# Two layers of decode attention and MLP: the streamed head pairs of a row grouped into one job of four

## The chip, the cores and the metric

One core of one Trainium2 chip. The metric is the device time of the kernel in microseconds (us). Executions of one kernel lie within about 0.5% of their median here. Before and after are compared with the runs that were taken beside each other. A program on one core has no second die to be compared with, so a run counts as fast when it lies within 1.5% of the fastest of its kernel.

## The reference

```python
W = min(4096, max(256, Sk // 4))           # 1024 of 4096 keys
q = (x @ wq).reshape(B, 1, 32, 128)        # 8 rows, 32 heads of 128, width 640
scores = einsum("bhqd,bhkd->bhqk", q, k[last W]) * 128 ** -0.5
o = einsum("bhqk,bhkd->bhqd", softmax(scores), v[last W])
attention = o.reshape(B, 1, 4096) @ wo

x = x + attention(layernorm(x))            # layer 1
x = x + mlp(layernorm(x))                  # 640 -> 1728, gelu, -> 640
x = x + attention(layernorm(x))            # layer 2: the SAME K and V, the same weights
x = x + mlp(layernorm(x))
```

Two things matter. The second layer reads the same K and V as the first, so whatever stays on the chip need not be loaded twice. And a row's second layer cannot begin before that row's first attention is complete and has gone through output projection, MLP, layernorm and query: a serial chain of small steps, once for each of the 8 rows.

## The kernel before

K or V of one *pair* of heads of one row is one unit of 128 x 2048 bf16 (512 KB). There are 27 unit buffers in SBUF. A row has 16 pairs, so 32 units; pairs 5 to 15 are kept for the second layer, pairs 0 to 4 are loaded again ("streamed"). Pair 5 is kept in PSUM instead of SBUF ("parked"), so 20 kept units lie in SBUF and 7 of the 27 buffers circulate.

```python
NUNIT = 27
STREAM = ((0, 3), (3, 5))                       # jobs whose K and V are loaded in both layers
KEEP = ((5, 8), (8, 12), (12, 16))              # jobs whose K and V stay for the second layer
PARK = {b: (('k', 5), ('v', 5)) for b in range(8)}
NOT = {}
WINDOWS = ("0:1a 0:1b 0:2a 0:2b", "1:0a 0:3a 0:3b", ..., "1:5a 1:5b 1:6a 1:7a 1:6b 1:7b")
ORDER = ( ... )                                 # a long string: the order in which all steps are emitted
```

A *job* is a group of up to four pairs that share one score bank, one exponent, one set of transposes and one set of folds. The tile `scr`, which takes the result of the exponent and later the sums of the folds, exists once for all jobs; the prediction calls it "the one score buffer". `WINDOWS[b]` lists the streamed jobs that are worked off while row b's chain runs ("1:0a" is layer 2, row 0, the first streamed job). The last window holds what waits for the last chain. In outline, one job is:

```python
def scores(job, i):      # 4 matmuls a pair; the K buffer comes free here, if it is not kept
    nc.tensor.matmul(job.s_ps[...], lhsT=view(low, ...), rhs=k[:, 512*a:512*a+512], ...)
    release(job, "k", i)
def exponent(job):       # one for the whole job
    nc.scalar.activation(scr[:], job.s_ps[:], ACT.Exp, scale=QSCALE)
def turn(job): ...       # 4 transposes (PE), then place() copies them (ACT), totals(), inverse()
def values(job, i):      # 4 matmuls a pair; the V buffer comes free here
    nc.tensor.matmul(job.o_ps[...], lhsT=view(misc, ...), rhs=v[:, 512*g:512*g+512], ...)
    release(job, "v", i)
def fold(job, t): ...    # 4 on DVE, then halve() twice, gathered() 2 matmuls, finish()
```

`chain(b)` is the MLP of row b, its layernorm and its queries. Every load is issued by one queue in a fixed order and waits until the next buffer of the free list is free.

The softmax here doesn't subtract the row's maximum and nothing guards it: scores larger than these inputs give would overflow.

Of the kernel before, what the change touches and what calls it, by code (L numbers as in the profile page):

```python
# [18 lines left out]
H = 32  # L19
# [3 lines left out]
F = 1728  # L23
EPS = 1e-5
QSCALE = DH ** -0.5
NKC = D // P
# [2 lines left out]

UNIT = 2048  # L30
NUNIT = 27
STREAM = ((0, 3), (3, 5))
KEEP = ((5, 8), (8, 12), (12, 16))
PARK = {b: (('k', 5), ('v', 5)) for b in range(8)}
ALSO = {}
NOT = {}
WINDOWS = ("0:1a 0:1b 0:2a 0:2b", "1:0a 0:3a 0:3b", "1:0b 1:1a 0:4a 0:4b", "1:1b 0:5a 0:5b", "1:2a 1:2b 0:6a 0:6b",
           "1:3a 1:3b 0:7a 0:7b", "1:4a 1:4b", "1:5a 1:5b 1:6a 1:7a 1:6b 1:7b")
WINDOWS = [[(int(w[0]), int(w[2]), ord(w[3]) - 97) for w in x.split()] for x in WINDOWS]
WPOS = (("w1", -1), ("w2", -1), ("wo", 8))  # L40
NHC = 13
HALF = F - NHC * P
ORDER = (
    "I))%(z<&2/,@/-%)%9yxyxyxyxyx2.z*z,z,z,y`y`y`z),,(4y[%yZyZyZ)zIy[y[yYyZyZyZyZyZyYyY&-(y[y[y]z9/&yTyT)+*(&(yRyqy"
    "RypyRyRyRyRyRyRyjyj&yVyXyVyYyYyYyYyYyYyYyYyYy]y]y]y]y_y_ykykyk{.{.yWyWyZyVyTyfyf{&yYyY{8yYyU{6yMyWyWyWyWyVy[y^"
    "y[y]y]%y_yU$#yQyQ$##yNyNyNzfzfyGyHyHyHyHyJyGyIyKz]yKz[z[yHyGzY#yFyFyFyFyFyFyF#z^yFyF$yMyDyDyDzVzgyDzHzH%yCzQzF"
    "%yByBzCzCzZyDyBzIzWzW#ziyAyAz>z>z>z>yAyAyAz`#z:y@y@y@zHz<$yAz8z9zCz3zRzBy?z2##z4y>z3z3z3y>z2z1z.z0z6y>#-&$z+yN"
    "z;z/z:z-yNy:z,y:yLyLy~&6)#z#z#z#z#z#z)y6yzy}y`y|/y5y}y~y~y5#y|yuyuyzyzyzyYy4yByUyUyByBysyryryr+yRypyRyq,##yOy2"
    "y2y2y;y;y0y1y9#%$#&y,yXy,y,y,y,y+y<y<yVy<y+y/y/y-yHyHy+yGy7#$#y*y*y2yDyGy*y*yBy*yXy*y&y)y,y,y>yjy,y)y+y+y)y*y8"
    "y8y8yIyIyIy8y]yHy*y*y*y3y/y*y(y)y)y0#%%##y#y,y,##y4y4y4y4y*y*x|y)x}y(x|y<y<y.y&y#$y$zVy$y6x~y&x}y3x~y$y$y$y/x~"  # L50
    "zJzJzJy#y#y,y#y#y#y#x}x~x~x~z?%y$zLx}x|##x|xzxzxzx}z4xzxzz2z?xzxzxzxzz;z.xzxzxzxz##z4xyxyxxz1xxz#xxz?x~y}y}$xx"
    "z)xwyzxwxwyxyxyxyxz1xyxwyzz.#y{xvxvxvxvyqxvyp#ys#&yoxsylynxsxvyvyvxvxsxsxt2$yfyoxnxqxqxqxqy&%y_y_y_y_y_$&#%yZ%"
    "#&y]xzxiyXxiyXxxxxxiyUyUyUyUy2yTyTxiy/y/xvxvxjxu%)yKxh-+xfxfxdy%y?y>x~y=xmxm$%xkx{x{y1y1y1xcxcxcxcxcxhxfxcxqxc"
    "y+yHxpxpxe#xdy)xdy($+xjxjxxxj$x~xwxaxa#xfy3y3xwx`x_x_%xcx^x^xqxazbxlx`x^x_xlxlxlx_x_x_x_x_zUxxxgx_x^xezP##&xb("
    "xcxYxmxWy#xZxXx_#xhxTxgx]x]x]x]x]x]xYxY#xoxoxoxo%x]xXx^x[xjxjx]x]x]x[z6xSxW#%xWz1xUxVxVxVxV#xZx]xTxTxTz%yrxWxX"
    "ypy}%#z0xRxQxQxQxQxQxTxMxPyrxPydz#xPxPxPxPxP#y`yixO#y[ytxNxNxNxNxNxNyVyVyVxNxKyZxM#yfyRyRyRyRyTxLxPySyPxLyQyZ$"
    "yYxNyOxKygygygxKyU#yLxK#xIxIyHyHyHyHyHyL#>&.$xDxDxDxDyCyAxGyAy>yJxGxDxDxEy7y7xE&yBxDxDy6y?y6y6y67y5y5xUxCy7xTx"
    "ky1y5y5*#&xQy,y/x@x@-+x|x|-#xzx<y$y$y$y$xJxJxJxJx|xwxxx_x_#x;&xrxyxYxsx;x;x;xUxoxVxUxpx;xCxCx7xexBx:x:*xMxMx?x"
    "9x9$####xYx4x4x6x3x1x@x4x4x4x2x3x;x;x;xOx;x3x3xzx3x3x3x3xHx6xtx5x3x4x4x3xVxBxBxBx;xRxRxRxRx3x3x3x>x3x3x3##)x9x"
    ";x0x:$xC#x6z,x-x5x?x?#x4x1x2xKxKxK#x,x0x0x0x0x0x4x/%x3x3x.x2ynx2x.x*x:%x9x,x8&yex7x-x-x&x,x,x2yKx+x+x+yHyHx+yj"  # L60
    "x+x-x-x+x,yBx/x*x*x*x*x*x*yIy;x*x*y9yE#yU###x%y4x%y>yNx%#yLx&x&x*yIx$x$x$x$x$y*y*y2$y)y)y)y)x(y,y(y(x#x&y%%w~w"
    "~x#w~x~x~x~x~y,x~x~x~y)w~-<9y%w{w{$wzwzxu,wy*xxwxwywywywywywywyxoxixgxhxhx/xjx/x/x/x/9wwxd##$x]x`x`wqx_zsx_x)x"
    "^x;wsxSzmzm)#$)%$wmw|wmzdwozcwmwmxNwmwmwmxMx,wuwuxA)#$wjxExGxG$wiwixqwiwiwiwkwywkwlwlwlwlwix9wvwsx7wux6x,wgx2w"
    "jwjwjwgwgxWwowox+whwhx:x+x-wgwgwgx%x###wfw|x#wgwgwuw|wuwgx?wzwzwzwzx#wgw~w~wyx6w}wvwgwfwv##*+wbwbwb#wq##)wnwnw"
    "nw^w^w]w]wgy<w]wdw]w`wtw]yVwa#y4#wbwbwZwawawkwkwkwkw^yHw`y(y(w`w`w`w`w^w_#w]y=wbw]w]w`w]w_wbw^wYw[w[w^xoxow[xn"
    "y-w]%y+wZ#y:xlwYwYwYwYxhw[xew[x{wYwYwbwYxa#y*x`x`x`x`x`x`$xawWwXx_wXwWx]wWx[x[xYwYxbwW#xWxWxWxWxWwWwVxhxZ###%3"
    "wQwQxNwQxQxOxMxZwQxNwQwQxVwSwSwQwRwRwRwRwRxDxD#xAxAxAxAxAxFxAx=wcwcxBx>xBxBx;wQ&wPw`w`w`)w_w_(3#0&$x<x2x;x1x,x"
    "-x/x/#wkx-x-x-wHwEwiwix)wgwgwUwUx(wGwHwHwHwGwG#(#%wKwywZwCwCwCwCwCwFwTwTwTwGwjwAwBwEwOwBwBwCw{wLwCwKwCwCwCwHw_"
    "wCwG+wRwWyMwGwGwBwBwBwD-wKwQwQwQwKwCwCwCwCwCwCw[w[$wZwZ&##*$w?w:wDwF#y?wAw;wC$#w7wJwJw9wIx}x}x}w=w>w>w>w>wF#w="
    "w=wAw=wAwAwAw;w?w<wHxkxkwH&w;()w:w6w9w9w3w8w8w7xlw7xkw;w;w7w:w7w6w2w4w4#w4w4w4w6w4w4xjw3w3w3w3w5w3w4w3xRxDx`w3"  # L70
    "w1xrw2w2x[x@w2xKxX#xWw1w1w2w1w1w1w1w1#%x5x5#w.xIw.w.x1w0x8w.xSx/x/x/x/x/x/x1w/w/x/w.#x-x-x+w-$#x)x)w+x(w+x&x;x"
    "+#w*w*xHx#x#x(x%w-w,w*#w{w}w(x,w)x+w{w(w($.%+x#w#wkwkw|w#w#w#wowowowowowmwn*$,()#w/w/wfwjwjwGwGw/wfqq#wcwCwCpw"
    "`w`w`w`w`w+w+$#w<w<nw(w(oow7wSwMoow#w#&w2vnnnwHnw-w-wE(#pw=lolnnlmmw9#(#rrrw3w5##hw2hhwDwDhhhhkkw*hvwQw(hiwNwN"
    "h%&&ueoeeow.eneew*w*nhejkll#ettiw1w1#rhhhegggcekkehdhh#c#oooeeeebjjbb_%#x+]]cccf]bb]]]#_wx_[#wuwuZZx(ZZZZ$#wmw"
    "mwmwzZZ^wj$]wiwiwrWWZWYWwlYwyWWw`whWXwf#w]w]w]w]w]VVV#)XwVwewZwXTTTTwUwRTTwRwRwRTwNwPwPwNwOwSTTTT%$$$$#)wD__MM"
    "MwBwBOO)Lw>MMUmw6UUw7UUMMwDMMMM(#$a^^w)JKw(w*w*]]u[KqrvvsuuZZw%ZKmppMKnLLL%###%DDw*MM#ZcccDDD]%CCCEGCDREESSSEE"
    "x1EB````OMDDDDKKKKJCGRRRDQGGGwq%#EBKKJDCCCCECDABDDBCA##$wW>>>>>wRwcwR@@wP>>>w[w[>wLwY###wI<wT<wHwHwH##::99wW:;"
    "wH$wSw?w?w?w?wE8w>w>88#7w<w:777w9788w6w6w68w:8888%)#)wvw*w+w+w+w+%/#)w&^^[[AA000r22(o;1/l08j0wV0-wU555FF/////]"
    "A[[[[00RRW0Q#(##$PPPO999LL#$&`$))F&((0CB0A0(((<(((99#)*&))333))))</--9...-)$($&(>(#&&&#88%%%@?F%J%%2E;(:1%#$$-"
    "-;$$$$$-$3#0&(++%+#*)$##$#")  # L80


class Job:
# [59 lines left out]
def _kernel(ctx: ExitStack, tc: tile.TileContext, A_small, A_k, A_v, A_wq, A_wo, B_w1, B_w2, out):  # L143
# [46 lines left out]
    xn = single["yT"]  # L190
# [30 lines left out]
    x0 = in_sb[:, 0:NKC * NB].rearrange("p (k b) -> p k b", b=NB)  # L221
# [365 lines left out]
    def add_job(job, early, rank0, ask=None, tail=False):  # L587
# [8 lines left out]
        def keep_apart(which, i, use):  # L596
            if job.layer == 0 and (which, i) in PARK.get(job.b, ()):
                for k in range(2):
# [4 lines left out]
        if job.layer == 1:  # L603
            src = twin(job)
            for w, i in PARK.get(job.b, ()):
                if i in pairs:
# [117 lines left out]

    held = {(w, i) for w in "kv" for i0, i1 in KEEP for i in range(i0, i1)}
    rows = []
    for b in range(NB):
        at, h = {}, (held | set(ALSO.get(b, ()))) - set(NOT.get(b, ()))
        rows.append([{part: [Job(b, layer, i0, i1, h, at) for i0, i1 in cut]
                      for part, cut in (("s", STREAM), ("k", KEEP))} for layer in range(2)])  # L730

# [8 lines left out]
    xn8 = narrow(NKC, NB, "xn8")  # L740
    _, _, r8 = layernorm(direct, x2, NB, lambda: xn8, False, "ln_r")
    q8_bank, q8_ps = bank(H, NB)
    for h in range(H):
        for kc in range(NKC):
            nc.tensor.matmul(q8_ps[:, h, :], lhsT=wq_sb[:, kc, h * DH:(h + 1) * DH],
                             rhs=xn8[:, kc, :], start=(kc == 0), stop=(kc == NKC - 1))
    nc.vector.tensor_tensor(out=qo, in0=q8_ps.rearrange("p h b -> p b h"), in1=r8()[:, :, None].to_broadcast([P, NB, H]),
                            op=ALU.mult)
    give(q8_bank)
# [16 lines left out]
    def late():  # L766
        first = asked[0]
        ends = []
        for part in range(len(STREAM) + len(KEEP)):
            at = [(x[1]["s"] + x[1]["k"])[part] for x in rows]  # L770
# [16 lines left out]
                         after=[d for d, h0, h1 in ends if h0 < h + 2 and h1 > h] + [head], take="park" if h == 0 else None)  # L787
            head = head or t

    jobs = rows[0][0]["s"] + rows[0][0]["k"]  # L790
    for b in range(NB):
        for layer, row, k in WINDOWS[b]:
            jobs = jobs + [rows[row][layer]["s"][k]]
        jobs = jobs + [job for job in rows[b][1]["k"] if any((w, i) not in job.held for w in "kv" for i in range(job.i0, job.i1))]
        jobs = jobs + (rows[b + 1][0]["k"] if b + 1 < NB else [])
# [7 lines left out]
    extra = {}  # L803
    for name, pos in WPOS:
        if pos < 0:
# [51 lines left out]
    y8 = narrow(NKC, NB, "y8")  # L857
# [43 lines left out]
```

## Time and profile before

| | before |
|---|---|
| time, median of the runs (their range) | 491.48 us (491.18 to 492.07) |
| span of the profiled execution | 488.7 us |
| PE busy | 392.6 us, 80% |
| DVE busy | 256.2 us, 52% |
| ACT busy | 76.4 us, 16% |
| loads on the queue | 191.13 MB, of which 336 units |
| last load lands / attention ends | 469.0 / 478.1 us |

The prediction shows the page's slices, the stretches, the landings and the groups. Three readings carry the rest: DMA moves 417 GB/s in nearly every slice, so the load stream is full; a few slices dip, all of them where a chain runs; and the last two slices have almost no loads (91 and 4 GB/s; the last one lands at 469.0), so something other than the loads fills the end.

### The profile page before, as it was taken

How to read it: one execution, taken by the hardware profiler on the slowest of the kernel's cores; microseconds unless marked ns; L12 is line 12 of the kernel's file. 1: busy time of each engine (PE TensorE's matmuls, PEld its weight loads, DVE VectorE, ACT ScalarE, POOL GpSimd, SP SyncE). 2: the span in 40 equal slices, each digit the busy share in tenths (PEclk: the TensorE clock that was granted, in tenths of full speed). 3: DMA queues.
4: the chain of work that ended last, by engine and by line, in shares of the span. 5: the costliest groups of instructions: out<-in, count | busy, mean ns of one | idle time of the engine just before them, and what ended most of it. 6: DMA issues, size and time to landing. Idle time of an engine off the chain costs nothing.

```text
span 488.7 us, 16784 instructions
## 1 busy us (share of the span) xinstructions
PE 392.6 (80%) x7201; PEld 212.3 (43%) x7201; DVE 256.2 (52%) x1116; ACT 76.4 (16%) x195; POOL 12.7 (3%) x24
## 2 busy tenths in 40 slices
PE   1412645998899998898989989988999899889985
PEld 0300124553365436542564355535552464365354
DVE  3001422455735764477454755666466746757563
ACT  1000000111211111112111211112112111121220
POOL 1000000000000000000000000000000000000001
PEclk9996555556655755557555575587556655765765
DMA  8999999999999999999999999999999999999920
GB/s 328 417 420 420 438 421 417 418 417 418 416 418 415 416 416 420 402 411 419 418 380 403 417 417 411 412 419 414 416 416 417 418 373 392 416 415 414 417 91 4
DMA packets 49898, 192.20 MB, mean 393 GB/s; under 512 B 5792, under 2 KB 5792, under 8 KB 48800
## 3 DMA queue, kind: packets, MB, share of 16 engines
q1 hardware_dynamic: 49824, 191.13, 96.5%
q8 instruction: 56, 0.92, 0.7%
q14 instruction: 18, 0.15, 0.1%
HBM read 191.10 MB, written 0.01 MB: 391 GB/s over the span
## 4 chain that ended last, share of the span: by engine, by line
PE 53%; DMA 21%; DVE 17%; issue 4%; ACT 3%; POOLq 0%; ACTq 0%; SPq 0%; DVEq 0%
PE s_ps L435 13%; PE o_ps L476 12%; DMA unit<-in_A_k_dram 9%; PE c_ps L536 6%; PE c_ps L698 6%; DMA unit<-in_A_v_dram 6%; DVE scr L486 5%; DMA wo_sb<-in_A_wo_dram 4%; PE c_ps L450 3%; PE c_ps L319 3%; PE o_ps L511 2%; PE c_ps L359 2%; PE c_ps L500 2%; DVE scr L484 2%; PE c_ps L273 1%
## 5 line engine op out<-in xcount | busy, mean ns | idle before, releaser
L435 PE MATMUL s_ps<-unit,low 128*1 128x512 bf16 (+3 forms) x1024 | 123.5, 564 | 18.9 <-DMA unit<-in_A_k_dram 13.2
L476 PE MATMUL o_ps<-unit,misc 128*8 128x512 bf16 (+3 forms) x888 | 108.2, 555 | 12.9 <-DMA unit<-in_A_v_dram 6.8
L444 ACT ACTIVATE scr<-s_ps 128x512 bf16<-128x512 f32 x80 | 47.8, 597 | 217.7 <-PE c_ps L500 127.9
L486 DVE SCALAR_TENSOR_TENSOR scr<-o_ps,low,scr 128x128 f32<-128x128 f32 x213 | 74.1, 348 | 5.9
L484 DVE TENSOR_SCALAR scr<-o_ps,low 128x128 f32<-128x128 f32 x71 | 24.7, 348 | 46.7 <-PE c_ps L450 30.1
L536 PEld LDWEIGHTS <-wo_sb 128*128 128x128 bf16 x1280 | 38.4, 103 | 21.5 <-issue 14.3
L435 PEld LDWEIGHTS <-low 128*1 128x1 bf16 (+3 forms) x1024 | 22.6, 91 | 50.3 <-issue 34.8
L698 PEld LDWEIGHTS <-wq_sb 128*128 128x128 bf16 x1280 | 38.0, 102 | 13.4 <-issue 12.6
L698 PE MATMUL c_ps<-low,wq_sb 128*128 128x1 bf16 x1280 | 40.8, 165 | 0.8 <-ACT misc L454 0.4
L454 ACT CAST misc<-c_ps 128x48 bf16<-128x48 f32 (+2 forms) x80 | 21.8, 272 | 123.0 <-DVE misc L465 22.1
L476 PEld LDWEIGHTS <-misc 128*8 128x8 bf16 (+3 forms) x888 | 20.2, 91 | 38.6 <-issue 27.1
L450 PEld LDWEIGHTS <-scr 128*128 128x128 bf16 x320 | 15.1, 104 | 39.9 <-ACT scr L444 35.7
L500 PEld LDWEIGHTS <-scr 128*128 128x128 bf16 x142 | 11.7, 105 | 39.1 <-DVE scr L495 12.2
L450 PE MATMUL c_ps<-misc,scr 128*128 128x16 bf16 x320 | 21.1, 176 | 8.7 <-ACT scr L444 5.7
L536 PE MATMUL c_ps<-misc,wo_sb 128*128 128x1 bf16 x630 | 19.8, 165 | 7.5 <-DMA wo_sb<-in_A_wo_dram 5.1
L465 DVE TENSOR_REDUCE misc<-c_ps 128x8 f32<-128x64 f32 (+2 forms) x80 | 16.0, 200 | 17.9 <-PE c_ps L460 11.6
L319 PEld LDWEIGHTS <-w_sb 128*128 128x128 bf16 x675 | 20.4, 104 | 9.9 <-issue 9.4
L460 PE MATMUL c_ps<-misc,low 128*128 128x48 bf16 (+2 forms) x80 | 16.5, 206 | 9.8 <-ACT misc L454 7.0
L500 PE MATMUL c_ps<-low,scr 128*128 128x8 bf16 x142 | 17.5, 176 | 7.6 <-DVE scr L493 3.3
L427 DVE CAST low<-c_ps 128x6 bf16<-128x6 f32 (+2 forms) x56 | 8.5, 154 | 28.0 <-ACT misc L454 16.9
L536 PE MATMUL c_ps<-low,wo_sb 128*128 128x1 bf16 x650 | 20.9, 165 | 2.3 <-DVE misc L465 1.4
L495 DVE TENSOR_TENSOR scr<-scr 128x128 bf16<-128x128 f32 x71 | 20.3, 286 | 2.4 <-PE s_ps L435 0.2
(98 smaller groups left out, 305.4 us busy)
## 6 DMA issues: line engine op xcount, KB each, us to landing
unit<-in_A_v_dram SPq DMA_DIRECT2D x168, 512.0 KB, 9.2
unit<-in_A_k_dram SPq DMA_DIRECT2D x168, 512.0 KB, 9.0
wq_sb<-in_A_wq_dram SPq DMA_DIRECT2D x5, 1024.0 KB, 8.9
wo_sb<-in_A_wo_dram SPq DMA_DIRECT2D x1, 5120.0 KB, 21.3
w_sb<-in_B_w_dram SPq DMA_DIRECT2D x1, 2176.0 KB, 25.1
w_sb<-in_B_w_dram SPq DMA_DIRECT2D x1, 2160.0 KB, 29.0
unit<-in_A_small_dram SPq DMA_DIRECT2D x1, 15.0 KB, 1.7
out_dram<-unit SPq DMA_DIRECT2D x1, 10.0 KB, 1.4
```

The costliest lines, as they stand in the source:

```text
L319: nc.tensor.matmul(t["h", k][1][:, fc - halves[k][0], :], lhsT=w_sb[:, kc * F + c0:kc * F + c0 + P], rhs=t["y"][:, kc, :], start=(kc == 0) ...
L435: nc.tensor.matmul(job.s_ps[32 * a:32 * a + r + 1, :], lhsT=view(low, job.qz + 5 + d - (d + 1) * r, (d + 1, r + 1)), rhs=k[:, 512 * a:512 ...
L444: nc.scalar.activation(scr[:], job.s_ps[:], ACT.Exp, scale=QSCALE)
L450: nc.tensor.matmul(job.t_ps[1][:, c], lhsT=scr[:, c * P:(c + 1) * P], rhs=small_ident.rearrange("p (a r) -> p a r", a=4), start=True, stop ...
L454: nc.scalar.copy(view(misc, 0, (64, job.n), (1, 4), (4, 4)), job.t_ps[1][:, :, :, 0:job.n].rearrange("p t a i -> p i a t"))
L476: nc.tensor.matmul(job.o_ps[32 * g:32 * g + 4 * r + 4, :], lhsT=view(misc, 48 * r + g, (4, 4 * r + 4)), rhs=v[:, 512 * g:512 * g + 512], s ...
L484: nc.vector.tensor_scalar(out=acc, in0=o[:, 0], scalar1=mask[:, 0:1], scalar2=None, op0=ALU.mult)
L486: nc.vector.scalar_tensor_tensor(out=acc, in0=o[:, t], scalar=mask[:, t:t + 1], in1=acc, op0=ALU.mult, op1=ALU.add)
L495: nc.vector.tensor_tensor(out=parts[:, 1], in0=acc, in1=parts[:, 0], op=ALU.subtract)
L500: nc.tensor.matmul(job.o8[1], lhsT=parts[:, h], rhs=sel, start=(h == 0), stop=(h == 1))
L536: nc.tensor.matmul(sums[1][:, n:n + 1], lhsT=wo_sb[:, h, n * P:(n + 1) * P], rhs=job.ot[:, h - 2 * job.i0:h - 2 * job.i0 + 1], start=(h == ...
L698: nc.tensor.matmul(job.q_ps[1][:, h - 2 * job.i0:h - 2 * job.i0 + 1], lhsT=wq_sb[:, kc, h * DH:(h + 1) * DH], rhs=xn[:, kc, :], start=(kc ...
```

## The change

Intent: one streamed job of four pairs instead of one of three and one of two, so 4 jobs for each row and layer, not 5 (64, not 80). With each job goes one exponent, one set of transposes, four folds and one gather. To keep the same number of units in SBUF, pair 5 now belongs to a kept job but is loaded again all the same, and pair 4 is kept in its place.

```diff
-STREAM = ((0, 3), (3, 5))
-KEEP = ((5, 8), (8, 12), (12, 16))
-PARK = {b: (('k', 5), ('v', 5)) for b in range(8)}
+STREAM = ((0, 4),)
+KEEP = ((4, 8), (8, 12), (12, 16))
+PARK = {b: (('k', 4), ('v', 4)) for b in range(8)}
-NOT = {}
-WINDOWS = ("0:1a 0:1b 0:2a 0:2b", "1:0a 0:3a 0:3b", ..., "1:5a 1:5b 1:6a 1:7a 1:6b 1:7b")
+NOT = {b: (('k', 5), ('v', 5)) for b in range(8)}
+WINDOWS = ('0:1a 0:2a', '0:3a', '0:4a 1:0a', '0:5a 1:1a', '0:6a 1:2a', '0:7a 1:3a', '1:4a', '1:5a 1:6a 1:7a')
+EARLY = [... for w in ''.split()]              # empty: no effect
 ORDER = ( ... )                                # another order string, cut here
@@ the first query, all rows at once
-    for h in range(H):
-        for kc in range(NKC):
+    for kc in range(NKC):
+        for h in range(H):
             nc.tensor.matmul(q8_ps[:, h, :], lhsT=wq_sb[:, kc, h * DH:(h + 1) * DH],
-                             rhs=xn8[:, kc, :], start=(kc == 0), stop=(kc == NKC - 1))
+                             rhs=xn8[:, kc, :], start=(kc == 0 and h == 0), stop=(kc == NKC - 1), skip_group_check=True)
```

The work after the last chain shrinks from six streamed jobs with 15 pairs to three with 12.

## The prediction

> **What bounds the kernel now.** I read the page's slices first, because they say by stage which resource is full.
>
> ```profile
> span 488.7 us, 16784 instructions
> ...
> PE   1412645998899998898989989988999899889985
> ...
> PEclk9996555556655755557555575587556655765765
> DMA  8999999999999999999999999999999999999920
> GB/s 328 417 420 420 438 421 417 418 417 418 416 418 415 416 416 420 402 411 419 418 380 403 417 417 411 412 419 414 416 416 417 418 373 392 416 415 414 417 91 4
> ```
>
> Each slice is 12.2 us. DMA is full in 37 of the 40 slices, at about 417 GB/s, and its queue carried 191.13 MB (part 3 of the page). 191.13 MB / 417 GB/s = 458.3 us: that floor does not move unless bytes do. Slices 17, 21 and 33 and 34 (402, 380, 373, 392) are dips, and the last two slices hold no loads: a tail. PE is nearly as busy as DMA, mostly at half clock, so it is the second resource. I looked at the dips in the stretches view (columns: stretch, length, busy time with instruction count of PE, PEld, DVE, ACT, POOL, granted clock, DMA share, GB/s):
>
> ```profile
> 85.00:95.00 10.00, 8.78 (x177) 5.45 (x177) 4.22 (x24) 1.05 (x4) 0.55 (x1) 0.50 1.03 417
> 195.00:205.00 10.00, 8.84 (x170) 5.33 (x166) 5.50 (x27) 1.44 (x5) 0.25 (x1) 0.50 1.02 401
> 245.00:255.00 10.00, 8.58 (x186) 5.67 (x185) 5.99 (x28) 1.41 (x5) 0.54 (x1) 0.50 1.00 373
> 255.00:265.00 10.00, 9.20 (x174) 4.92 (x173) 4.19 (x24) 0.60 (x2) 0.54 (x1) 0.50 1.01 400
> 395.00:405.00 10.00, 9.20 (x203) 6.17 (x204) 5.37 (x30) 1.32 (x5) 0.63 (x2) 0.50 0.98 360
> 405.00:415.00 10.00, 10.00 (x180) 4.73 (x181) 5.64 (x23) 2.02 (x5) 0.45 (x1) 0.58 1.02 396
> 447.00:470.00 23.00, 20.76 (x325) 9.01 (x323) 16.25 (x67) 4.86 (x12) 0.15 (x1) 0.72 0.89 360
> ```
>
> Lost against 417: 0.38 + 1.06 + 0.41 + 1.37 + 0.50 = 3.7 us. That is all the middle has to give. The dips lie in the chains (row b's MLP and queries between its two layers), and the time from issue to landing in the dip (second line) against the stretch before it (first) shows why: the queue runs shallow because free buffers are short.
>
> ```profile
> DMA to landing us min/median/max: 8.8/9.9/10.0
> DMA to landing us min/median/max: 5.4/6.6/9.1
> ```
>
> The end, from the view in order of time:
>
> ```profile
> 469.06 0.60 PE L435 MATMUL s_ps<-unit,low 128*1 128x512 bf16 x4 [0.34 <-DMA unit<-in_A_k_dram]
> ...
> 478.13 0.22 DVE L854 TENSOR_TENSOR unit<-park,low 128x40 f32<-128x40 f32 x1 [0.85 <-PE park L760]
> ```
>
> The last load lands at about 469.0. Attention runs to 478.1 (9.1 us more), and the MLP of all rows and the store take 10.6 us to 488.7.
>
> **What the Trainium skill says.** "Perfetto Trace Analysis", section "Identifying Performance Opportunities", says to work on the most contended engine within each regime, to judge DMA by memory traffic rather than by occupancy, and that repeated bubbles on the engine that should be full can mean too few buffers. The trace agrees: 417 GB/s in the middle, and dips with 5.4 us landings where 9.9 is the full queue. "DMA: Bandwidth & Descriptors", "Where 436 GB/s comes from", puts the fabric ceiling at 435 GB/s; 417 is 96% of it, so no faster middle is to be had. "TensorE: Matmul & The Clock Gate", Part 1, says that an idle array sits at half clock and that activity frees it. The trace does not agree: 85 to 95 us is 88% busy at 0.50, while the first slices, one to four tenths busy, show 0.9. So I count on no clock gain from the change.
>
> **What the change does to bytes and buffers.** Before: pairs 5 to 15 kept (22 units), pair 5 of them parked in PSUM, pairs 0 to 4 loaded again, 10 loads per row. After: pairs 4 to 15 without 5 (22 units), pair 4 parked, pairs 0 to 3 and 5 loaded again, 10 loads per row. Both load 8 x (32 + 10) = 336 units and keep 20 in SBUF, so 7 of 27 circulate. The floor of 458.3 us stays.
>
> **What it removes.** Jobs go from 80 to 64. A job costs, by the groups in the page:
>
> ```profile
> L444 ACT ACTIVATE scr<-s_ps 128x512 bf16<-128x512 f32 x80 | 47.8, 597 | 217.7 <-PE c_ps L500 127.9
> L486 DVE SCALAR_TENSOR_TENSOR scr<-o_ps,low,scr 128x128 f32<-128x128 f32 x213 | 74.1, 348 | 5.9
> L484 DVE TENSOR_SCALAR scr<-o_ps,low 128x128 f32<-128x128 f32 x71 | 24.7, 348 | 46.7 <-PE c_ps L450 30.1
> L454 ACT CAST misc<-c_ps 128x48 bf16<-128x48 f32 (+2 forms) x80 | 21.8, 272 | 123.0 <-DVE misc L465 22.1
> L495 DVE TENSOR_TENSOR scr<-scr 128x128 bf16<-128x128 f32 x71 | 20.3, 286 | 2.4 <-PE s_ps L435 0.2
> ```
>
> DVE: 4 x 0.348 + 0.286 + 0.222 (its cast) + 0.40 (sum and reciprocal) + 0.31 (query copy and finish) = 2.6 us; 16 fewer make 42 of 256 us. ACT: 0.60 + 0.27 = 0.87, 14 of 76 us. PE: transposes 0.27, totals 0.20, gathering 0.20 to 0.40, some 0.75; 12 of 393 us. Matmuls over K and V do not change (256 pair-steps each). In the middle all of this lies beside the loads; it pays only where it keeps a buffer from being freed late: at most the 3.7 us.
>
> **The start.** The loop over the first query is turned so that four fifths of its 160 matmuls run while wq still arrives; 156 of them took 4.3 us after the last piece (15.9 us). The first scores come at some 17.7 instead of 21.1 us. DMA share is 1.0 there and 27 units can be loaded before one must be free: worth about 0.
>
> **Cover of the chains.** I read the emitted order out of the two order strings and followed the free list first in, first out. For each row's chain I counted the loads between the last one of its first layer and the first one whose buffer is freed by the chain's own first scores:
> before, rows 0 to 7: 19, 18, 20, 17, 18, 20, 17, 18;
> after: 15, 15, 18, 18, 19, 19, 15, 17.
> One load is 0.524 MB / 417 GB/s = 1.26 us. The two 17s of before are rows 3 and 6, and just these made the big dips (1.5 and 1.9 us); 18 and more gave 0 to 0.4. After has three 15s, as a window with one streamed job has only 7 + 8 units. Two loads less are 2.5 us less cover. Against it, the chain is shorter with fewer other jobs in between: before, row 3's took 13.4 us from its entry (243.95) to its first scores (257.39); with no turn, totals or folds between it I estimate 11.5 to 12.5 from the same lines. Net: rows 0, 1 and 6 lose 0.5 to 2.5 each, the dips of rows 3 and 6 as they were go. I take 4.7 us of dips against 3.7: **+1.0 us**.
>
> **The tail.** The loads after the last chain's last first-layer load number 26 against 29, so the chain ends 3 x 1.26 = 3.8 us nearer to the last landing. Before: first scores of row 7 at 447.5, attention done at 478.1, 30.6 us, with PE busy 27 of them and the one score buffer taken by 7 exponents (1.1 us with transpose) and 7 folds (2.6), 26 us: both nearly full. After: 4 exponents and 5 folds, 17 us; PE loses 5 pair-steps of 0.4, 3 transposes, 3 totals, 2 gathers, gains 32 short columns (1.0) and 4 heads of queries (0.6): about 25.5 us in all. Attention ends at -(26 x 1.26) + 14.5 + 25.5 = 7.3 us after the last landing, against 9.1: **-1.8 us**. The very last load is a V of a kept job, which still needs values (1.0), folds (1.4), halves (0.5), gather and finish (0.5) and eight heads of the output (1.3): 4.7 plus handoffs, so it doesn't bind.
>
> Sum: +1.0 - 1.8 = -0.8 us on the span; on the measured 491.2 that is 490.4. I shade it to **490.0**, since a shorter DVE and ACT load can only help release buffers.
>
> **Rivals.** (1) Starved chains: rows 0, 1 and 6 each lose the full 2.5 us and the rest stay: +5 us, 495 to 496. For it: the two 17s dipped. Against: 58 us of the queue's waiting is for values already, and those come earlier with less DVE work. (2) Dips vanish: PE and DVE relieved, all 3.7 us come back and the tail gives 2 to 3 more: 485. For it: PE is 88 to 100% busy in every dip. Against: the cover counts. (3) The loads set the end and nothing else moves: 489 to 491.5, as bytes are equal. For it: DMA at 417 in 37 slices. Slower by over 2% needs 10 us of dips, which no cover here explains; faster by over 2% needs 9.8, more than 3.7 plus any likely tail.
>
> **Range and chances.** Rival 1 at one side and 2 at the other give 485.5 to 494.5. Faster by over 2%: 0.05; within: 0.92; slower: 0.03.
>
> **What would show it.** Right: 336 loads again, jobs' exponents x64 and folds x165 + 55, DVE down by about 40 us, DMA at 417 with dips in rows 1 and 6 and none in row 3, attention ending 6.5 to 8 us after the last landing, first scores near 17.7 with nothing gained. Wrong: a middle without dips (cover is not what counts, PE's work is), a tail over 10 us (the last job of four or the last chain binds), or slices well under 400 GB/s in several chains.

## The result, and the profile after

After: 488.68 us (488.35 to 489.34) against 491.48: 2.8 us less. The ratio is 0.9943, with a 95% interval of 0.9926 to 0.9961. Here and below a ratio compares the fast runs of two kernels in the same rounds, so it is not quite the ratio of the medians that are quoted. In the four batches of experiments the kernel before had medians of 490.35 to 491.26, and the unchanged after had 488.68 again where it ran, 1.7 us less than before beside it; so the gain is about 2 us. The profiled spans differ by 2.1 us.

The page's slices of the kernel after (12.2 us each):

```profile
span 486.6 us, 16342 instructions
PE 374.7 (77%) x7113; PEld 208.5 (43%) x7113; DVE 221.2 (45%) x947; ACT 63.1 (13%) x155; POOL 12.7 (3%) x24
...
PE   3113654899689798988889888979998788989885
...
PEclk9999999998655865568556675585558755775875
DMA  8999999999999999999999999999999999999940
GB/s 327 418 420 420 446 417 414 418 417 419 415 405 378 419 415 417 418 416 418 418 415 419 416 417 416 407 418 418 414 403 418 418 403 353 411 417 416 418 165 3
```

DVE lost 35 us of work, ACT 13, PE 18, and the span lost 2.1. PE also waits longer for loads now: the idle time before its score matmuls that a K load ended is 36.4 us, and it was 13.2 before (part 5 of the page). The dips have moved: slices 17, 21 and 33 to 34 before, now slices 12 to 13, 30 and 33 to 34. Taken over slices 7 to 37, what is missing to 417 GB/s is 156 GB/s-slices before and 161 after, and 161 / 417 x 12.2 us = 4.7 us against 4.6: the middle came out even.

The groups of the jobs of the kernel after (columns: line, engine, operation, out from in, shapes, count, busy time and ns of one, idle time before them and what ended it):

```profile
L439 ACT ACTIVATE scr<-s_ps 128x512 bf16<-128x512 f32 x64 | 38.2, 597 | 237.9 <-PE c_ps L495 128.7
L481 DVE SCALAR_TENSOR_TENSOR scr<-o_ps,low,scr 128x128 f32<-128x128 f32 x165 | 57.6, 349 | 4.8
L479 DVE TENSOR_SCALAR scr<-o_ps,low 128x128 f32<-128x128 f32 x55 | 19.1, 348 | 63.1 <-PE o_ps L471 36.4
```

Each operation costs what it cost before (597 and 348 ns); there are just fewer: 64 exponents for 80, 220 folds for 284.

The granted clock has to be read with care. The trace's first clock record comes at 105.8 us in after and at 41.4 us in before, and the views show 1.00 until then. The score matmuls say otherwise; these lines give count, duration in ns (min/median/max), and first and last start, for 20 to 105 us of after and for 460 to 476 us, where the records give 0.74:

```profile
L430 PE MATMUL s_ps<-unit,low x128: 582/631/634, 24.5 to 104.7; 128*4 128x512 bf16 x32, 128*3 128x512 bf16 x32, 128*2 128x512 bf16 x32, 128*1 128x512 bf16 x32
L430 PE MATMUL s_ps<-unit,low x28: 378/379/380, 462.0 to 465.8; 128*3 128x512 bf16 x8, 128*2 128x512 bf16 x8, 128*1 128x512 bf16 x8, 128*4 128x512 bf16 x4
```

In before the same matmuls took 583 to 634 ns at a recorded 0.50 (140 to 160 us). So the 1.00 of the first 105 us is a gap in the record and not a fast clock, and the mean clock of a whole execution, which counts the gap as 1.00, isn't to be compared between runs.

The stretches of the kernel after (same columns as in the prediction):

```profile
85.00:95.00 10.00, 8.47 (x177) 5.51 (x176) 2.26 (x14) 0.92 (x3) 0.00 (x0) 1.00 1.03 417
140.00:155.00 15.00, 13.47 (x261) 7.89 (x261) 5.41 (x31) 2.12 (x6) 0.54 (x1) 0.50 0.99 374
355.00:360.00 5.00, 4.93 (x76) 2.47 (x77) 2.83 (x17) 0.00 (x0) 0.54 (x1) 0.50 1.01 387
395.00:405.00 10.00, 8.89 (x192) 5.64 (x188) 5.61 (x25) 1.22 (x4) 0.54 (x1) 0.50 1.00 389
405.00:415.00 10.00, 9.16 (x156) 4.66 (x156) 3.16 (x16) 1.29 (x3) 0.54 (x1) 0.50 0.95 344
447.00:470.00 23.00, 19.57 (x414) 11.08 (x412) 14.80 (x63) 5.04 (x12) 0.54 (x1) 0.80 0.90 364
```

Row 1's chain (140 to 155 us) and row 6's (395 to 415) are short of loads now, row 3's (245 to 265 before) no longer. In row 1's dip the time from issue to landing shrinks as it did in the dips before; first the stretch before it (130 to 140 us), then the dip:

```profile
DMA to landing us min/median/max: 7.1/10.3/10.3
DMA to landing us min/median/max: 4.6/6.7/9.6
```

From the view in order of time of the kernel after, the start and the end (start, length, what, count, idle time before and who ended it):

```profile
17.29 1.01 PE L740 MATMUL park<-unit,wq_sb 128*128 128x8 bf16 x32 [2.63 <-DMA wq_sb<-in_A_wq_dram]
24.50 1.02 PE L430 MATMUL s_ps<-unit,low 128*4 128x512 bf16 x8 [6.19 <-DMA unit<-in_A_k_dram]
...
475.97 0.22 DVE L849 TENSOR_TENSOR unit<-park,low 128x40 f32<-128x40 f32 x1 [1.44 <-PE park L755]
```

The first query is done early, as meant, and then PE waits 6.2 us for a K unit: the first scores come at 24.5 us, not at 17.7 (in before they came at 21.1). The new order starts with the job of pairs 0 to 3, and the K of its pair 0 is the sixth unit in the queue and lands at 24.46 us; before's first scores used pair 3, second in the queue. Attention ends at 476.0 against 478.1.

**Where the gain came from.** The stretch from the last chain's first scores to the end of attention, before:

```profile
447.90:478.10 30.20, 26.92 (x517) 14.46 (x513) 19.00 (x83) 6.38 (x16) 0.00 (x0) 0.67 0.65 263
```

and after:

```profile
450.90:476.00 25.10, 21.60 (x511) 13.16 (x507) 15.98 (x66) 4.14 (x10) 0.00 (x0) 0.77 0.66 269
```

The end of attention is the sum of three times, read from the trace (landings counted in the order of the queue):

| | before | after | difference |
|---|---|---|---|
| last load of row 7's first layer lands | 431.97 (load 307) | 435.21 (load 310) | +3.24 |
| from there to the first scores of its second layer (the chain) | 15.95 | 15.66 | -0.29 |
| from there to the end of attention | 30.21 | 25.10 | -5.11 |
| end of attention | 478.13 | 475.97 | -2.16 |

The chain starts later since three loads more stand before it in the queue, and the work behind it is shorter. Load by load the two kernels run level: load 97 lands 0.9 us later after, load 145 0.1 later, load 289 0.9 earlier, load 326 at the same time. Two traces of the unchanged after differ by as much: in the second (after_again) load 310 lands at 435.96 us and the end stretch takes 24.9.

The chains themselves, rows 1 to 7 (row 0 is left out, as the weights are loaded during its chain): time from the row's last first-layer landing to its chain's first scores, and the number of loads that can be issued meanwhile without a buffer from that chain (its cover, 1.26 us each):

| row | 1 | 2 | 3 | 4 | 5 | 6 | 7 |
|---|---|---|---|---|---|---|---|
| before: us | 16.7 | 19.5 | 17.6 | 18.0 | 18.0 | 17.6 | 15.9 |
| before: cover | 18 | 20 | 17 | 18 | 20 | 17 | 18 |
| after: us | 14.9 | 16.6 | 17.1 | 18.0 | 16.4 | 15.7 | 15.7 |
| after: cover | 15 | 18 | 18 | 19 | 19 | 15 | 17 |

Chains: 114.4 against 123.3 us, 8.9 less. Cover: 121 loads against 128, so 7 x 1.26 = 8.8 us less. In sum the shorter chains were paid back in cover, nearly to the last tenth. Cover x 1.26 less the time is the spare of a row. Loads were lost where it is smallest: rows 3 and 6 before (3.8 us each) and rows 1 and 6 after (4.0 and 3.2): 1.5 to 2.4 us in each. Rows with 4.7 us or more lost at most 0.4, so a row seems to need some 5 us of spare, and not just more than none, for the queue to stay full.

### The profile page after: what moved, and what is told of

It reads as the page before. It is cut to its first block, busy times and chain, and to the rows that moved or that the text cites. A ratio compares the mean times of both kernels' runs of the same rounds, so it can differ in the third digit from the quotient of the medians.

```text
span 486.6 us, 16342 instructions
## 1 busy us (share of the span) xinstructions
PE 374.7 (77%) x7113; PEld 208.5 (43%) x7113; DVE 221.2 (45%) x947; ACT 63.1 (13%) x155; POOL 12.7 (3%) x24
## 3 DMA queue, kind: packets, MB, share of 16 engines
q1 hardware_dynamic: 49824, 191.13, 96.9%
## 4 chain that ended last, share of the span: by engine, by line
DMA 47%; PE 38%; DVE 10%; issue 2%; ACT 2%; SPq 0%; POOLq 0%; ACTq 0%; DVEq 0%
DMA unit<-in_A_k_dram 32%; DMA unit<-in_A_v_dram 12%; PE s_ps L430 10%; PE o_ps L471 8%; PE c_ps L693 6%; DMA wq_sb<-in_A_wq_dram 3%; PE c_ps L354 3%; PE c_ps L314 2%; DVE scr L481 2%; PE c_ps L531 2%; PE o_ps L506 1%; PE c_ps L445 1%; PE c_ps L268 1%; DVE scr L479 1%; PE park L755 1%
## 5 line engine op out<-in xcount | busy, mean ns | idle before, releaser
L430 PE MATMUL s_ps<-unit,low 128*2 128x512 bf16 (+3 forms) x1024 | 116.8, 535 | 46.3 <-DMA unit<-in_A_k_dram 36.4
L471 PE MATMUL o_ps<-unit,misc 128*4 128x512 bf16 (+3 forms) x880 | 102.6, 526 | 10.3 <-ACT misc L449 4.8
L481 DVE SCALAR_TENSOR_TENSOR scr<-o_ps,low,scr 128x128 f32<-128x128 f32 x165 | 57.6, 349 | 4.8
L430 PEld LDWEIGHTS <-low 128*2 128x2 bf16 (+3 forms) x1024 | 24.2, 91 | 80.6 <-issue 55.5
L479 DVE TENSOR_SCALAR scr<-o_ps,low 128x128 f32<-128x128 f32 x55 | 19.1, 348 | 63.1 <-PE o_ps L471 36.4
L693 PEld LDWEIGHTS <-wq_sb 128*128 128x128 bf16 x1280 | 37.0, 101 | 12.2 <-issue 12.1
L471 PEld LDWEIGHTS <-misc 128*4 128x4 bf16 (+3 forms) x880 | 20.8, 94 | 35.9 <-issue 18.9
L449 ACT CAST misc<-c_ps 128x64 bf16<-128x64 f32 x64 | 19.2, 300 | 93.9 <-PE c_ps L445 29.1
L407 DVE TENSOR_SCALAR unit<-park 128x512 uint32<-128x512 uint32 x32 | 21.1, 680 | 7.9 <-PE o_ps L471 5.5
L314 PEld LDWEIGHTS <-w_sb 128*128 128x128 bf16 x675 | 20.2, 104 | 9.3 <-issue 9.2
L398 DVE TENSOR_SCALAR park<-unit 128x512 uint32<-128x512 uint32 x32 | 21.5, 683 | 3.6 <-DMA unit<-in_A_v_dram 3.6
L531 PE MATMUL c_ps<-misc,wo_sb 128*128 128x1 bf16 x640 | 18.9, 164 | 4.9 <-DMA wo_sb<-in_A_wo_dram 2.7
L354 PEld LDWEIGHTS <-w_sb 128*128 128x128 bf16 x585 | 17.5, 104 | 10.7 <-issue 8.3
L506 PE MATMUL o_ps<-misc,unit 128*128 128x1 bf16 x576 | 18.6, 165 | 3.0 <-DVE scr L481 1.5
L506 PEld LDWEIGHTS <-unit 128*128 128x128 bf16 x576 | 17.4, 102 | 7.9 <-DMA unit<-in_A_v_dram 5.1
## 6 DMA issues: line engine op xcount, KB each, us to landing
wo_sb<-in_A_wo_dram SPq DMA_DIRECT2D x1, 5120.0 KB, 21.1
w_sb<-in_B_w_dram SPq DMA_DIRECT2D x1, 2176.0 KB, 24.5
```

The source lines that it names most:

```text
L314: nc.tensor.matmul(t["h", k][1][:, fc - halves[k][0], :], lhsT=w_sb[:, kc * F + c0:kc * F + c0 + P], rhs=t["y"][:, kc, :], start=(kc == 0) ...
L354: nc.tensor.matmul(t["o", k][1][:, n, :], lhsT=w2_sb[:, fc * D + n * P:fc * D + (n + 1) * P], rhs=t["g", k][:, fc - f0, :], start=(fc == f ...
L398: nc.vector.tensor_scalar(out=job.parked[which, i][k][:].bitcast(U32), in0=u[:, 1024 * k:1024 * k + 1024].bitcast(U32), scalar1=0, scalar2 ...
L430: nc.tensor.matmul(job.s_ps[32 * a:32 * a + r + 1, :], lhsT=view(low, job.qz + 5 + d - (d + 1) * r, (d + 1, r + 1)), rhs=k[:, 512 * a:512 ...
L471: nc.tensor.matmul(job.o_ps[32 * g:32 * g + 4 * r + 4, :], lhsT=view(misc, 48 * r + g, (4, 4 * r + 4)), rhs=v[:, 512 * g:512 * g + 512], s ...
L479: nc.vector.tensor_scalar(out=acc, in0=o[:, 0], scalar1=mask[:, 0:1], scalar2=None, op0=ALU.mult)
```

## The experiments

Theory, from the prediction: the load stream sets the pace; the middle depends on cover and on chain length; job work in the middle lies beside the loads and costs nothing; the start is worth nothing; the gain is the shorter work after the last chain. Rivals: job work in the middle is not hidden (it holds buffers), or the last landings set the end. All kernels were timed in five rounds. Quoted times of before: 490.35 us in the first batch, 491.26 in the second, 490.76 in the third, 490.94 in the last.

### after_again: the yardstick

The changed kernel with no edit, run beside the experiments.

> The changed kernel once more, as the yardstick of this call. All theories: 0.994 to 0.995 of the kernel before, some 488.5 to 489.0 us; attention ends about 8 us after the last load lands.

488.68 us (488.47 to 489.52), ratio 0.9969 [0.9956, 0.9982]; attention ends at 476.05 us. Differences below are taken from this median. The batches ran on three chips, and before's median differs by up to 0.9 us between the batches, so I read nothing into differences under 1 us. The unchanged kernel itself has ratios of 0.9943 and 0.9969 in its two sets of runs.

### start_old: undo the turned query loop

```diff
-    for kc in range(NKC):
-        for h in range(H):
+    for h in range(H):
+        for kc in range(NKC):
```

> The changed kernel with the old loop order of the first query (heads outside, pieces of wq inside). Theory (the loads have 27 free buffers there, so an earlier first score frees nothing that is waited for): first scores about 3 us later, time within 0.5 us of the changed kernel. Rival (the earlier start is what was gained): 1.5 to 3 us slower than the changed kernel, back at the kernel before.

489.10 us (488.62 to 489.4), ratio 0.9973 [0.9959, 0.9987]. No effect on the time, as predicted, but not for the reason given: the first scores came at 24.67 us, as in after_again, and not 3 us later. With either loop they wait for the K of pair 0 (it lands at 24.63 here). So in the new order the turned loop is hidden behind that load, and the run does not show what an earlier first score would be worth.

### dup_mid: the softmax and fold work of the streamed jobs, doubled

In the 13 streamed jobs outside the last window every exponent, transpose, copy, total, fold, halving and gather is issued twice; the result does not change.

```diff
+    def times(job):
+        late = job.layer == 1 and job.b >= 5
+        return 2 if job.i0 == 0 and not late else 1
-        nc.scalar.activation(scr[:], job.s_ps[:], ACT.Exp, scale=QSCALE)
+        for _ in range(times(job)):
+            nc.scalar.activation(scr[:], job.s_ps[:], ACT.Exp, scale=QSCALE)
 ...  # the same for turn, place, totals, inverse, fold, halve, gathered
```

> The changed kernel with the softmax, totals, fold and gather instructions of 13 streamed jobs (all but those of rows 5, 6 and 7 in the second layer) issued twice, with the same result: the instructions that the change removed are back, with buffers, loads and order as changed. Theory (in the middle the loads set the pace and job overhead lies beside them): vector engine busy some 30 us more, time within 0.7 us of the changed kernel, dips in rows 1 and 6 as they were or a little deeper. Rival (a relieved vector and tensor engine is what helps, by freeing buffers earlier): 2 us or more slower, with new dips in several rows.

509.19 us (505.74 to 510.54), ratio 1.0372 [1.0342, 1.0402]: 20.5 us more, where the theory allowed 0.7. From its page:

```profile
PE 379.7 (75%) x7204; PEld 212.1 (42%) x7204; DVE 251.4 (50%) x1051; ACT 74.7 (15%) x181; POOL 12.7 (3%) x24
...
GB/s 328 418 419 420 430 432 415 415 419 418 416 333 349 416 418 416 359 398 418 417 353 377 419 417 392 329 413 418 413 369 404 417 354 294 400 416 416 414 152 3
```

DVE is busy 50% of the span, less than before's 52%, and still six chains starve (333 and 349, 359, 353 and 377, 329, 369, 354 and 294). Their times grow by 2.9, 3.1, 4.4, 3.6, 2.3 and 4.9 us (rows 1 to 6), 21 us together, and the landings fall behind with them: against after_again 2.9 us at load 97, 17.2 at the last. So "job work in the middle lies beside the loads" fell for added work: the steps of a window's jobs are emitted between the steps of the row's chain, and what is put there lengthens the chain, here by its measured 21 us. A share of busy time says nothing against that. The doubled work is that of ACT, DVE and PE together; the run does not part them.

### dup_tail: the same in the last window's three streamed jobs

The same edit with `late` in place of `not late`.

> The same doubling for the other three streamed jobs alone (rows 5, 6 and 7 of the second layer, those of the last window). Theory (work after the last chain sets the end): two folds, two gathers and two or three softmaxes more on the one score buffer, 1 to 3 us slower than the changed kernel, the last load landing at the same time and attention ending later by that much. Rival (the last landing sets the end): within 0.4 us.

497.45 us (496.98 to 497.99, four fast runs), ratio 1.0145 [1.0128, 1.0162]: 8.8 us more. Stretch from the last chain's first scores to the end of attention:

```profile
452.80:485.00 32.20, 27.12 (x521) 14.56 (x517) 21.21 (x83) 5.34 (x13) 0.00 (x0) 0.50 0.49 189
```

32.2 us for 25.1, so 7.1 of the 8.8 us arise here, more than the 1 to 3 that I expected; and the last load, which was to land unmoved, landed 2.8 us later (470.85). The clock is 0.50 in this stretch for 0.77 in the unchanged one, so part of it may be slower matmuls; the run does not part the two. With the unchanged instructions at 0.56 (units_26 below) the stretch took 26.9 us, so the clock is probably the smaller part.

### long_1, long_5, long_7: one row's chain made longer

The hidden matmuls of one row's MLP are issued twice (an estimated 2.35 us more in the chain), for row 1, 5 or 7.

```diff
-            for fc in range(f0, f1):
+            for fc in rounds * list(range(f0, f1)):
-        closed = mlp(step, x2s, x2s[:, 1], 1, x2s[:, 0])
+        closed = mlp(step, x2s, x2s[:, 1], 1, x2s[:, 0], 2 if b == 1 else 1)   # or 5, or 7
```

> The changed kernel with the first MLP matmuls of row 1's chain issued twice (75 more, same result, about 2.35 us at 31 ns). Theory (spare of a chain = its cover in loads x 1.26 us less the time from the last first-layer landing to the chain's first scores; loads are lost as soon as the spare is under about 5.5 us): row 1 has 15 x 1.26 - 14.9 = 4.0 us and lost 1.5; with 2.35 us less it loses 2.0 to 2.6 us more, and the whole kernel is that much slower. Rival (chains are hidden, the loads go on): under 0.5 us.

491.45 us (491.13 to 492.16), ratio 1.0007 [0.9991, 1.0024]: 2.8 us more. Row 1, with 4.0 us of spare, was already losing loads and had none to give: its chain grew by 2.0 us, loads landed some 3 us later than in after from there on (1.8 to 3.1 later than in after_again) and never made it good. As the theory said, though 2.8 is a little above its 2.0 to 2.6.

> The same in row 5's chain. Theory: row 5 has 19 x 1.26 - 16.4 = 7.5 us to spare, 5.1 after; 0 to 0.7 us slower, at most a slight dip. Rival 1 (any lengthening of a chain costs its length, cover or not): 2.35 us slower. Rival 2 (hidden): 0, as for row 1.

490.84 us (490.19 to 491.45), ratio 0.9989 [0.9972, 1.0007]: 2.2 us more, where I had expected 0 to 0.7 for a row with 7.5 us of spare. The chain grew by 3.2 us and the issues of loads 251 to 260 slipped by 3.4 to 3.6; their landings slipped by only 1.0 to 1.6 (all against the trace of after; against after_again 2.5 to 2.9, and 0.5 or less), so the queue's reserve took up about 2 us. But row 6, the row with the least spare, then lost about 2 us more. A queue that enters a tight row with less reserve pays there. That is how I read the size that I missed: spare is not a property of one row alone. (Rival 1, which let any lengthening cost its length, had named 2.35 us; by its reason the loss should have come in row 5.)

> The same in the last chain (row 7, 17 loads, spare 5.7 us, 3.3 after). Theory (work after the last chain sets the end, not the last landing): last landing 1.5 to 2.3 us later, first scores of row 7 and the end of attention both 2.0 to 2.7 us later, whole kernel 2.0 to 2.7 us slower. Rival (the last landing sets the end and the chain is hidden): 0 to 0.5 us.

491.70 us (491.35 to 492.52), ratio 1.0013 [0.9996, 1.0029]: 3.0 us more. The chain grew by 2.9 us, the last landing came 3.6 later and the end of attention 3.1 later. Both moved together, so this run does not tell which of them sets the end.

### last_columns: no folds in the last kept job

The last kept job gives its result by single columns (128x1 matmuls) instead of by wide matmuls and folds.

```diff
-            part1(job, False, (), base, ask(...))
+            part1(job, b + 1 == NB and job is rows[b][1]["k"][0], (), base, ask(...))
```

> The changed kernel with the very last job (pairs 4 to 7 of row 7, second layer, whose V is the last load) taking its values column by column as the last streamed job does: 64 short matmuls of 31 ns (2.0 us) in place of 16 wide ones (1.9), and no folds (1.5), halves (0.5) and gather (0.3) before its finish. Theory (that job's chain after the last landing sets the end): attention ends about 2 us earlier, 1.5 to 2.3 us faster than the changed kernel, the loads unmoved. Rival (the tensor engine's remaining output matmuls set the end): within 0.7 us, as those 80 take 2.5 us after it.

488.56 us (488.0 to 489.27), ratio 0.9949 [0.9932, 0.9966]: within the unchanged kernel's two ratios and 0.1 us off its median, not the 1.5 to 2.3 us better that I had expected. The last job was done at 473.2 us, earlier than the 474.4 of the changed kernel, but 140 output matmuls still stood in PE's queue and ran to 476.8. From this run's own first scores of row 7 (451.67 us) to the end of attention it took 25.2 us with PE busy 22.4; in after_again it took 24.9 with 22.9. So 1.7 us less DVE work in the stretch shortened nothing.

### early_gather: last_columns, and a part of the output matmuls moved forward

The output matmuls of heads 24 to 31 are emitted ahead of the last streamed job's values.

```diff
-        for h in range(0, H, 2):
+        for h in [*range(24, H, 2), *range(0, 24, 2)]:
```

> The version with columns for the last job, and with the output matmuls of heads 24 to 31 (40 of 160) moved ahead of the last streamed job's values, where the tensor engine idled 0.75 us. Theory (after the last landing the tensor engine is the bound, which is why columns alone gave nothing): attention ends 0.6 to 1.3 us earlier than with columns alone, 487.3 to 488.0 us. Rival (something else, such as the last V's arrival, sets the end): no change from 488.6.

488.89 us (488.09 to 489.18), ratio 0.9958 [0.9941, 0.9974]; attention ends at 476.7; the stretch took 24.95 us with PE busy 22.9. No gain: moving this part of PE's work about within the stretch does not shorten it.

### units_26: one buffer fewer

The changed kernel with 26 unit buffers. The order of every engine's instructions is identical.

```diff
-NUNIT = 27
+NUNIT = 26
```

> The changed kernel with 26 buffers in place of 27; the order on every engine is the same, instruction for instruction, so only the cover of each chain is one load (1.26 us) less: 14, 14, 17, 17, 18, 18, 14, 16. Theory (cover decides the dips): rows 1 and 6, which already dip, lose about 1.26 us more each, rows 2, 3, 4 and 7 0.3 to 1 us each, 3 to 6 us slower in all, with the loss seen as landings that fall behind in the chains. Rival (the dips come from the tensor engine's work in the chain, not from buffers): within 1 us.

494.46 us (491.52 to 496.32), ratio 1.0071 [1.0042, 1.01]: 5.8 us more. From its page:

```profile
GB/s 328 417 420 420 439 420 418 418 416 417 417 373 365 418 415 401 382 416 419 416 413 413 419 417 404 397 418 417 414 410 418 418 375 319 419 414 406 414 123 3
```

The dips sit where they sat (slices 12 to 13 and 33 to 34), deeper, with a new one in slices 16 and 17. The chains are as long as they were (14.9, 16.6, 17.1, 17.9, 16.3, 15.7, 15.4 us). With no instruction moved, one of the seven circulating buffers is worth more than twice what the change gained. So it is cover that is short in the chains, as the theory said (3 to 6 us).

### before_light: the jobs' work taken out, the order left

The kernel *before*, with the 16 second streamed jobs (pairs 3 and 4) stripped of their exponent, transposes, copy, three of four folds and the halving. The result is wrong; every other step stays in its place in the order.

```diff
-        nc.scalar.activation(scr[:], job.s_ps[:], ACT.Exp, scale=QSCALE)
+        if job.i0 != 3:
+            nc.scalar.activation(scr[:], job.s_ps[:], ACT.Exp, scale=QSCALE)
 ...  # the same for turn, place, folds 1 to 3, halve
```

> The kernel before with the second streamed job of each row (pairs 3 and 4) stripped of its exponent, transposes, copy of the weights, three of four folds and the halves (the result is wrong on purpose): 16 jobs lose most of their own work while buffers, loads, order and cover stay as before. Theory (less job work at the old cover is what the change would have given had it not paid in cover): chains 1 to 2 us shorter, the dips of rows 3 and 6 mostly gone, tail shorter by two jobs' work; 5 to 8 us faster than the kernel before, so 3 to 5 us faster than the change. Rival (job work in the middle is hidden; only the tail gains): 2 to 3 us faster than the kernel before, dips unchanged.

490.51 us (488.77 to 492.26), ratio 0.9996 [0.9973, 1.0019]: nothing, where even the rival had said 2 to 3. From its page:

```profile
PE 390.9 (80%) x7137; PEld 209.9 (43%) x7137; DVE 235.5 (48%) x1041; ACT 64.2 (13%) x163; POOL 12.7 (3%) x24
...
GB/s 327 418 419 421 431 427 418 419 416 419 417 416 417 419 416 412 402 416 417 416 386 405 416 418 399 413 418 418 410 407 419 417 369 383 417 413 404 414 84 4
```

DVE lost 20.7 us and ACT 12.2, most of what the change took from them (35 and 13), but PE only 1.7 of 18. The profiled run was the slowest of the six. The dips stand where they stood in before: slice 17 (402), 21 and 22 (386, 405), 33 and 34 (369, 383). The chain times are 16.3, 19.9, 17.7, 18.6, 19.3, 18.9 and 15.8 us, not shorter. The stretch at the end took 29.6 us for 30.2. So it is not the jobs' work on DVE and ACT whose removal paid in the change; for PE's share this run says little.

### skip_last: the last ten loads left out

The changed kernel without the ten loads of row 7's second layer; the buffers keep what was in them, so the result is wrong (the comparison passed, so it is too coarse to see this). All other instructions have the same order on their engines.

```diff
-        nc.sync.dma_start(units[s][:], (A_k if which == "k" else A_v)[job.b, i])
+        (job.layer, job.b) == (1, 7) or nc.sync.dma_start(units[s][:], (A_k if which == "k" else A_v)[job.b, i])
```

> The changed kernel with the last ten loads (row 7's second layer: K and V of pairs 0 to 3 and 5) left out; the buffers keep what was in them, so the result is wrong on purpose. Every engine but the one that issues loads has the same instructions in the same order. The last landing should fall from 468 to about 455.6 us. In every run of the changed kernel so far (dup_tail apart) attention ended 7.4 to 8.0 us after the last landing. Theory A (the work that is left after the last chain sets the end, the last landings lie beside it): first scores of row 7 at about 451 and attention done within 1 us of 476, so some 20 us after the last landing; time 487.5 to 489. Theory B (the last landing sets the end, the work follows it): attention done 4 to 12 us earlier, time 477 to 485. In between (1 to 4 us earlier): both bind in turn, and the K landings at 462 are the likely place.

488.67 us (488.15 to 489.56), ratio 0.9962 [0.9944, 0.9979]: the same. The last landing comes at 456.05 us for 468.05. The view in order of time, in the changed kernel:

```profile
465.18 1.04 PE L430 MATMUL s_ps<-unit,low 128*4 128x512 bf16 x16
...
470.04 1.89 PE L471 MATMUL o_ps<-unit,misc 128*16 128x512 bf16 x16
...
474.18 1.75 PE L755 MATMUL park<-wq_sb,wo_sb 128*128 128x8 bf16 x60
```

and in skip_last:

```profile
465.78 1.04 PE L430 MATMUL s_ps<-unit,low 128*4 128x512 bf16 x16
...
470.50 1.89 PE L471 MATMUL o_ps<-unit,misc 128*16 128x512 bf16 x16
...
474.65 1.75 PE L755 MATMUL park<-wq_sb,wo_sb 128*128 128x8 bf16 x60
476.43 0.22 DVE L849 TENSOR_TENSOR unit<-park,low 128x40 f32<-128x40 f32 x1 [1.44 <-PE park L755]
```

Scores, values and output matmuls of the last job start 0.5 to 0.6 us later, not earlier, though their K and V have no loads to wait for. That small shift was there before: row 7's last first-layer load landed at 435.74 us for 435.21. From its first scores at 451.3 us to the end it took 25.1 us, as in the changed kernel. So in the changed kernel the last ten landings do not set the end; the work behind the last chain does. (The kernel before was not tested so.) This also explains a puzzle of the other runs: in every version of the changed kernel but the doubled ones (dup_mid 8.8, dup_tail 14.2) attention ended 7.4 to 8.0 us after the last landing, which looks like a wait for it. Both hang on a third thing, row 7's last first-layer landing: 26 loads follow it at one pace, and a chain and 25 us of work follow it at another.

## Why the prediction was right or wrong

**The class and the time: right.** 490.0 was predicted, in 485.5 to 494.5; 488.68 was measured. Within 2%, as expected.

**The floor: right.** The queue carries the same 191.13 MB at 417 GB/s, and 35 us less DVE work bought no faster load.

**What is removed: right in count, high in size.** Exponents x64, folds x165 + 55. DVE lost 35 us, not 42: the folds gave 22.1 (74.1 + 24.7 - 57.6 - 19.1), the small steps 13 where I had put 20. PE lost 18 us, not 12: 12.3 of them lie in the groups of wide matmuls on K and V (123.5 + 108.2 - 116.8 - 102.6), which I had counted as unchanged; their number is all but the same (1024, and 880 for 888), and their mean fell from 564 to 535 and from 555 to 526 ns.

**The start: right on the worth, wrong on the time.** Nothing was gained (start_old), but the first scores came at 24.5 us and not at 17.7: I followed the query and not the order of the first K loads behind it. So the worth was right partly by luck: the earlier start that was to be worth nothing never came about.

**Cover and dips: the places right, the balance off.** Row 3's dip is gone and rows 1 and 6 dip, as counted; row 0, with 15 loads of cover, does not. The count had left out the three loads of wo, w1 and w2 (5120, 2176 and 2160 KB), which stand in the queue between row 0's last first-layer unit, which lands at 62.2 us, and the next unit, which lands at 85.9, so row 0's cover is over 20 us longer than 15 loads. The step that failed is the term "+1.0 us" for the middle: it came out even (load 310 lands 0.4 us earlier than in before, in after_again 0.3 later). The 4.7 us of dips that I gave to after are what its slices show. I had summed before's losses over a few stretches, 3.7 us; its slices 7 to 37 give 4.6. And I had let chains get shorter by an estimated 1 to 2 us in row 3 alone; they got shorter by 1.7, 2.9, 0.5, 0, 1.5, 1.9 and 0.3 (rows 1 to 7).

**"In the middle all of this lies beside the loads": half right, and for a weaker reason than I gave.** Taken out in place, on DVE and ACT, it gains nothing (before_light). Put in, it costs its full length (dup_mid). What shortened the chains in the change is, I argue, the new order with fewer other steps between those of the chain (PE's share of the work is the rival that before_light leaves); no run here shows that by itself, since one can't reorder the old jobs without making another plan.

**The tail: the mechanism and the main size right, the size partly by luck.** Predicted from the last chain's first scores to the end 25.5 us, measured 25.1 (before 30.2; the prediction's 30.6 starts at 447.5, the first score matmul at 447.92). But the terms that it lists for PE come to only some 2.4 us less (2.0 + 0.8 + 0.6 + 0.6 - 1.0 - 0.6). Taken from PE's 27 us this leaves 24.6, and 25.5 then needs PE's idle time to fall from 3.6 us to 0.9, for which it gives no sum. In the traces the idle time hardly moved (3.3 us before, 3.5 after) and PE's busy time fell by 5.3. In the three times of the table above I had predicted +4.8 for the landing (3.8 for three loads, 1.0 for the middle), -0.5 for the chain and -5.1 for the work, -0.8 in all; measured +3.2, -0.3 and -5.1, so -2.2. The miss lies in the first: in before's own stream loads 307 to 310 take 3.7 us (435.63 - 431.97), and after load 310 lands 0.4 us earlier than before, where I had put 1.0 later. Rival 3, that the loads set the end, is refuted by skip_last. What fills the 25.1 us is not settled. Between the two profiled executions PE's busy time fell by 5.3 us and the stretch by 5.1 (its wide matmuls on K and V are 136 for 156 and took 15.7 for 20.2 us), which would fit PE as its bound. But part of that is the clock, 0.77 for 0.67 in this stretch: in after_again, at 0.71, PE fell by 4.0 us and the stretch by 5.3:

```profile
451.14:476.05 24.91, 22.86 (x511) 13.60 (x507) 16.06 (x65) 4.15 (x10) 0.00 (x0) 0.71 0.67 273
```

And with the same instructions PE was busy from 21.6 us (after) to 24.1 (dup_mid), while the stretch kept to 24.9 to 25.5 us in all runs but dup_tail and units_26. So neither PE's busy time nor the clock alone explains its length. Less DVE work gave nothing (last_columns), more work of all three engines cost 7 us (dup_tail), and no run took only PE's work away: that the fewer pairs and jobs shorten the stretch is read off the two kernels, and by which engine stays open.

**No gain from the clock: it can stay, but one ground for it was a misreading.** That the first slices show 0.9 while PE is hardly busy is the gap in the record told of above: in before it lasts to 41.4 us, and the score matmuls in it took 584 to 631 ns, as at 0.50. The other ground holds: 85 to 95 us of before was 88% busy at a recorded 0.50. The mean clocks of whole executions, 0.612 before and 0.721 after, differ in good part by the lengths of the gaps, and before's times do not follow them: 490.76 us at 0.616 and 490.62 at 0.694 in the same batch.

## What to carry to other kernels

Ask of an operation not whether its engine is busy but whose queue position it holds: doubled in place in the chains, softmax and fold work cost 20.5 us with DVE 50% and ACT 15% busy, and taken out of the same kind of place on these two it gained nothing, I think because the order around it stayed. When loads are full, a chain's price is its length less the loads that can run under it, and here a change that shortened both by the same 9 us broke even. And to learn whether a last transfer sets the end, leave it out: a constant distance between the two may only mean that both follow a third event.

## What the Trainium skill lacked or had wrong

- "DMA: Bandwidth & Descriptors", "Where 436 GB/s comes from": it says that between HBM and SBUF the HBM side, about 358 GB/s for a core, binds. The runs differ: 417 GB/s from HBM in most slices of both kernels, with one core at work. The measurement decides. The same passage calls a measured 425 GB/s for one 16 MB load "near fabric-rate", and that is what the runs come near to; so the passage has both figures, and what it says binds is not what bound one core here. One slice in each kernel shows more than its 435 GB/s for the fabric (438 before, 446 after), which no run here explains.
- "TensorE: Matmul & The Clock Gate", Part 1: that activity releases the half clock does not describe these traces, if the busy time of the views is what the page means by activity. In before, PE was busy 18.91 of the 20 us from 140 to 160 us, at a recorded 0.50 throughout, with score matmuls of 583 to 634 ns. The page warns in general of such records; it does not say that a record can start late (at 41.4 us before, 105.8 us after) and then reads as 1.00.
- "Perfetto Trace Analysis", "Identifying Performance Opportunities": its remark on repeated bubbles and too few buffers holds (one buffer of 27 fewer: 5.8 us more), but it gives no way to see it coming. In these traces the time from issue to landing shows the queue's reserve: a median of 9.9 and 10.3 us at a full queue, of 6.6 and 6.7 us in the dips, where single landings fell to 5.4 and 4.6. A shorter time alone is no dip: from 285 to 295 us of before the median was 6.7 and the least 5.8, at 418 GB/s.
- No page that I read for this tells of added work that lengthens a chain by its position in the queues of engines that are far from full (13 jobs' softmax and folds doubled: 20.5 us, with DVE 50%, ACT 15% and PE 75% busy).
